# Pair-by-pair loads, earlier product pieces and rest tokens turned together in a fused attention and SwiGLU kernel

## The chip, the cores and the metric

One NeuronCore of a Trainium2 chip runs the whole program. The metric is device time in microseconds (us) from launch to end. TensorE (PE; PEld is its weight load), VectorE (DVE), ScalarE (ACT), GpSimd (POOL) and SyncE (SP) each run their own instructions in order and wait for each other through semaphores. POOL, SP and ACT issue the DMA transfers.

## The reference

Attention over 8 batches of 12 heads, 448 tokens and 64 values per head; then a SwiGLU block over all 3584 tokens:

```python
scores = scale * np.matmul(q, k.transpose(0, 1, 3, 2))
attn = softmax(scores)                      # over the last axis
attn_out = np.matmul(attn, v)               # (8, 12, 448, 64)
x = attn_out.transpose(0, 2, 1, 3).reshape(3584, 768)
g = x @ w_gate                              # (3584, 1536)
out = (g / (1 + exp(-g)) * (x @ w_val)) @ w_out   # (3584, 768), float32
```

## The kernel before

**Tiles.** Two heads make a pair, six pairs a batch, 48 pairs in all (`NHP` = 6, `NPAIR` = 48). The 448 tokens of a head lie as four chunks (`NC`) of 112 partitions (`P`): token 4p + c is row p of chunk c. Queries, keys, values and weights are brought to 16 bits by the load. A *unit* is one chunk of keys of one pair: two score matmuls into a PSUM tile of two banks (`s`) and one exponential of both heads into `E` (`qk`, L213).

**Turning queries and keys.** `prep` (L158) brings a pair's queries and keys into `qkT`, with the 64 values of a head along the partitions. Keys take 448 columns, queries 448 more, and the first 64 query columns are repeated at the end, so that the two heads can read the queries in different rotations (head 0 from column S + D, head 1 from column S). For pair 0 this is done by matmuls against the identity, for pairs 1 to 10 by 16 TensorE transposes and two VectorE copies (L207, L210), from pair 11 on (`NPE`) by DMA transposes on SP from a POOL copy.

**Product with the values.** `pv_chunk` (L229) makes one *piece*: eight matmuls of one chunk of `E` with the values of that chunk, which have a column of ones behind them, so the sums of the softmax come with the product. The product `acc` has seven blocks of 128 rows by 65 columns. In the first six each, 128 tokens of one head; the seventh holds the remaining 64 tokens (the *rest tokens*) of both heads, one head in each half of the partitions. After the fourth piece VectorE takes the reciprocals (L264) and scales into `xt` (L265). For the seventh block, from pair 12 on (`XPE`), two extra VectorE operations (L274) put the halves side by side for the DMA transpose.

**Turning the product.** `turn_x` (L282) turns `xt` into columns of `X`, the input of the FFN (768 rows in six blocks, 896 tokens of two batches). For pairs 0 to 11: three matmuls of 128 columns (L292), two of 64 columns for the rest tokens (L296), and one VectorE copy of 448 columns (L303). For later pairs: two DMA transposes. In `X` the rest tokens of a batch are its first 64 columns.

**FFN.** `ffn1_steps` makes one *visit* per block of 128 hidden columns (12 of them): six matmuls for the gate, a tanh on ScalarE, six matmuls for the value, two VectorE operations (L336, L339). `ffn2_steps` multiplies with `w_out`, ScalarE copies the result to `osb` (L369) and SP writes it out, row piece by row piece (L381), since the order of the tokens in `X` isn't that of the output. In the very last chunk ACT issues the pieces under 64 rows. A block of the FFN is the first 384 columns of an `X` tile, or the other 512.

**PSUM.** `ps_s` has three tiles of two banks, for scores, most gates and the turns of pairs up to 7; `ps_f` has two tiles of one bank, for products, the other turns, the FFN's value side and output, and one gate in visits that have no product. A tile is taken in a ring, so an instruction waits until the tile's user before last is read out.

**Order.** It is written out by hand, each engine keeping the order of the program. The prologue is a loop of 24 units, batch 0's pairs 0 to 5. In it stand the turns of later pairs, loads put into lists by pair (`wq`, issued at the second unit of a pair), value copies (`copy_v`), dummies that keep TensorE at work, pieces from unit 8 on, and `turn_x` of pairs 0 to 3 at the units of `XAT`. Then the loop over `plan` mixes two or three units, products of pairs whose exponentials are made, and FFN visits. The first step makes the last pieces of batch 0 and starts the FFN; the FFN of batch 1's tokens and the rest tokens of batch 0 belong to the second block.

**Loads.** All but the first pair's go through POOL (L127 queries and keys, L134 values, L151 and L153 weights). Each has one of eight semaphores in turn: a load is issued when the load eight earlier has landed. Batch 0's queries and keys are loaded one pair at a time for pairs 1 to 3 and two at a time later, values three pairs at a time:

```python
load_qk16(3, 1)
load_v(0, GP)
load_qk16(4)
load_v(3, GP)
```

Of the kernel before, what the change touches and what calls it, by code (L numbers as in the profile page):

```python
# [23 lines left out]
WIDE = 8  # L24
XPE = 12
NE = 4
NX = 3
NV = 6
VS = 6
EB = 15  # L30


# [1 line left out]
def kernel(  # L34
# [21 lines left out]
    GPB = NHP // GP  # L56
    sm_scale = float(D) ** -0.5
    OH = DM // 2

    tabs = list(get_activation_tables(nc.m.arch).keys())  # L60

# [19 lines left out]
    ps_f = ctx.enter_context(tc.tile_pool(name="ps_f", bufs=2, space=PSUM))  # L81

    Es = [consts.tile([P, NC * EB + 1, D], FP16, name=f"E{i}") for i in range(NE)]
    Xts = [consts.tile([128, 4, 128], FP16, name=f"xt{i}") for i in range(NX)]
    Vts = [consts.tile([P, 2, NC, D + 2], FP16, name=f"vo{i}") for i in range(NV)]
    vraw = consts.tile([P, VS, 2, NC, D], FP16, name="vraw")
    warm = consts.tile([128, 512], FP16, name="warm")
# [51 lines left out]
    def copy_v(pr):  # L139
        nc.vector.tensor_copy(Vts[pr % NV][:, :, :, 0:D], vraw[:, pr % VS])  # L140

# [13 lines left out]
    def prep(pr):  # L155
        rq, rk = raw[pr]
        if pr == 0 or pr >= NPE:
            qk16 = attp.tile([P, 2, NC, 2, D], FP16, tag="qk16", bufs=3)  # L158
            for t, src in enumerate((rq, rk)):
                dst = qk16[:, 1 - t].rearrange("p c h d -> p h c d")  # L160
                if pr == 0:
                    nc.vector.tensor_copy(dst[:, 0], src[:, 0])
                    nc.scalar.activation(dst[:, 1], src[:, 1], AF.Copy)
                else:
                    nc.gpsimd.tensor_copy(dst, src)  # L165
        qkT[pr] = attp.tile([128, 2 * S + D], FP16, tag="qkT", name="qkT", bufs=5)
        if pr >= NPE:
            nc.sync.dma_start_transpose(
                qkT[pr][:, 0 : 2 * S].rearrange("p (c q) -> p c q", q=P),
                qk16[:].rearrange("p t c h d -> p (t c h d)"),  # L170
            )
            nc.sync.dma_start_transpose(
                qkT[pr][:, 2 * S :].rearrange("p (c q) -> p c q", c=1),
                qk16[0:D, 1, 0].rearrange("p h d -> p (h d)"),
            )
            return None

        def turn0():
            for t in range(2):
                tp = ps_s.tile([128, 2, 512], FP32, tag="s", name="tp")  # L180
                for c in range(NC):
                    for hx in range(2):
                        nc.tensor.matmul(
                            tp[ts(hx, 64), c // 2, ds(c % 2 * P, P)],
                            lhsT=qk16[:, 1 - t, c, hx],
                            rhs=ident[0:P, 0:P],
                            start=True,
                            stop=True,
                        )
                dst = qkT[pr][:, ts(1 - t, S)].rearrange("p (a x) -> p a x", a=2)  # L190
                nc.vector.tensor_copy(dst[:, 0], tp[:, 0, 0 : 2 * P])
                nc.scalar.activation(dst[:, 1], tp[:, 1, 0 : 2 * P], AF.Copy)
                if t == 0:
                    tq = tp
            nc.vector.tensor_copy(qkT[pr][:, 2 * S :], tq[:, 0, 0:D])  # L195

        def turn():
            if pr < FIRST + 2:
                tp = ps_s.tile([128, 2 * NC, 256], FP16, tag="s", name="tp")
            else:  # L200
                tp = ps_f.tile([128, 2 * NC, 128], FP16, tag="f", name="tp")
            for t in range(2):
                for c in range(NC):
                    for hx in range(2):
                        src = raw[pr][t][:, hx, c, :]
                        nc.tensor.transpose(tp[ts(hx, 64), (1 - t) * NC + c, 0:P], src, ident[0:P, 0:P])  # L206
            nc.vector.tensor_copy(  # L207
                qkT[pr][:, 0 : 2 * S].rearrange("p (c q) -> p c q", q=P), tp[:, :, 0:P]
            )
            nc.vector.tensor_copy(qkT[pr][:, 2 * S :], tp[:, NC, 0:D])  # L210

        return turn if pr else turn0

# [22 lines left out]
    def pv_chunk(pr, c):  # L236
        if c == 0:
            accs[pr] = ps_f.tile([128, 512], FP32, tag="f", name="acc")
        e = Es[pr % NE]
        vo = Vts[pr % NV]  # L240
        a7 = accs[pr][:, 0 : 7 * (D + 1)].rearrange("p (s d) -> p s d", s=7)
        for j in range(3):
            for hx in range(2):
                nc.tensor.matmul(  # L244
                    a7[:, 2 * j + hx],
                    lhsT=e[:, ds(c * EB + 9 * hx + 2 * j, 2)].rearrange("p b x -> p (b x)"),
                    rhs=vo[:, hx, c, 0 : D + 1],
                    start=c + j + hx == 0,
                    stop=False,
                )  # L250
        for hx in range(2):
            nc.tensor.matmul(  # L252
                a7[:, 6],
                lhsT=e[:, ds(c * EB + 6 + hx, 2)].rearrange("p b x -> p (b x)"),
                rhs=vo[:, hx, c, 0 : D + 1],
                start=False,
                stop=c == NC - 1 and hx == 1,
            )
        if c < NC - 1:
            return  # L260
        r = attp.tile([128, 8], FP32, tag="R", bufs=2, name="R")
        xt = Xts[pr % NX]
        n = 7 if pr < XPE else 6
        nc.vector.reciprocal(r[:, 0:7], a7[:, :, D])  # L264
        nc.vector.tensor_tensor(  # L265
            xt[:].rearrange("p j (h d) -> p (j h) d", h=2)[:, 0:n],
            a7[:, 0:n, 0:D],
            r[:, 0:n].unsqueeze(2).to_broadcast([128, n, D]),
            ALU.mult,
        )  # L270
        if pr < XPE:
            return
        for hx in range(2):
            nc.vector.tensor_scalar(  # L274
                xt[0:D, 3, ts(hx, D)], a7[ts(hx, D), 6, 0:D], r[ts(hx, D), 6:7], None, ALU.mult
            )

    def pv(pr):
# [3 lines left out]
    def turn_x(pr):  # L282
# [6 lines left out]
        if pr < XPE:  # L289
            tp = accs[pr] if pr < FIRST else ps_f.tile([128, 512], FP32, tag="f", name="xtp")  # L290
            for j in range(3):
                nc.tensor.matmul(  # L292
                    tp[:, ds(D + 128 * j, 128)], lhsT=xt[:, j], rhs=ident[:], start=True, stop=True
                )
            for hx in range(2):
                nc.tensor.matmul(  # L296
                    tp[ts(hx, D), 0:D],
                    lhsT=xt[:, 3, 0:D],
                    rhs=ident[:, ts(hx, D)],
                    start=True,  # L300
                    stop=True,
                )
            nc.vector.tensor_copy(dst, tp[:, 0:S])  # L303
            return
        nc.sync.dma_start_transpose(
            dst[:, D:S].rearrange("p (j q) -> p j q", j=3), xt[:, 0:3].rearrange("p j m -> p (j m)")
        )
        nc.sync.dma_start_transpose(dst[:, 0:D].rearrange("p (j q) -> p j q", j=1), xt[0:D, 3])

    gate_small = [False]  # L310

# [32 lines left out]
    def ffn2_steps(kk, c0, n, hts, first, last_block):  # L344
# [6 lines left out]
        for ch, oh in steps:  # L351
# [7 lines left out]
            for m0, w in parts:  # L359
# [15 lines left out]
                l = l0  # L375
                while l < l0 + 128:
                    b, j = divmod(l, S)
                    c, p0 = divmod(j, P)
                    m = min(P - p0, l0 + 128 - l)
                    eng = nc.scalar if last and m < 64 else nc.sync  # L380
                    eng.dma_start(  # L381
                        out[ts(NB * kk + b, S), :].rearrange("(p c) m -> c p m", c=NC)[
# [13 lines left out]
    with tc.manual_schedule():  # L396
# [4 lines left out]
        for vo in Vts:  # L401
            nc.vector.memset(vo[:, :, :, D:], 1.0)
        load_qk16(1, 1)
        make_identity(nc, ident)
        load_qk16(2, 1)
        load_qk16(3, 1)
        load_v(0, GP)
        load_qk16(4)
        load_v(3, GP)
        dummy(7)  # L410
        prep(0)()
# [2 lines left out]

        wq = {
            0: [("qk", 6), ("g", 0), ("v", 0)],
            1: [("qk", 8), ("g", 1), ("v", 1)],
            3: [("qk", 10), ("V", 2), ("g", 2), ("v", 2)],
            4: [("g", 3), ("v", 3), ("qk", 12)],
            6: [("V", 3), ("o", 0)],  # L420
            7: [("o", 1)],
# [30 lines left out]
        def run_o():  # L452
            gen, t = oq.pop(0)
            next(gen)
            return t
# [9 lines left out]
        def share(total, at, n):  # L465
            return (at + 1) * total // n - at * total // n

        XAT = (11, 15, 17, 20)
        pieces = [(p, c) for p in range(FIRST) for c in range(NC)]

        def piece():
# [2 lines left out]
        for u in range(FIRST * NC):  # L474
# [9 lines left out]
                prep(2)()  # L484
            elif u >= 6 and c == 2:
                prep(pr + 2)()
            if u in (5, 6, 7):
                dummy(1)
            if u in (6, 14):
                for p in range(3):  # L490
                    copy_v(u // 8 * 3 + p)
            if c == 1:
                for w in wq.pop(pr, []):
                    emit(w)
            if u in XAT:
                turn_x(XAT.index(u))
            for _ in range(1 if c == 2 or u in XAT else 2):
                if u >= 8 and pieces[0][0] * NC + pieces[0][1] <= u - 3:
                    piece()

        queue = []
# [24 lines left out]
        for x, (chunks, todo) in enumerate(plan):  # L526
# [40 lines left out]
            else:  # L567
# [16 lines left out]
                        run_fv()  # L584
                for _ in range(no):
                    run_o()
            while turns:
                turn_x(turns.pop(0))
        run_budget(1e9)
        oq.extend(ffn2_wait)  # L590
        ffn2_wait.clear()
# [36 lines left out]
```

The softmax here doesn't subtract the row's maximum and nothing guards it: scores larger than these inputs give would overflow.

## Time and profile before

| what | value |
|---|---|
| median of 5 runs (lowest to highest) | 454.06 us (453.71 to 455.16) |
| the profiled execution, its own time | 455.1 us |
| its span, first to last instruction | 453.3 us |
| granted TensorE clock, mean | 0.999 |
| exponentials (L226), 192 | 162.6 us busy |
| FFN gate, value and output matmuls | 124.7, 124.7 and 116.1 us busy |
| products (L244 and L252) | 53.0 and 42.9 us busy |
| scores (L218), 384 matmuls | 50.5 us busy |
| DMA moved | 48.71 MB, mean 107 GB/s |

The share of busy time of an engine is an average over stages that differ: in the first 32 us there is no FFN, in the last 20 no attention. So the timeline is read stage by stage: an engine that is idle shows, in brackets behind its next instruction, for how long and what ended it. The start of a group of equal instructions and the start of the next group give what the first group costs; the printed duration of matmuls includes the way through the array and overlaps with what follows. The landing of a transfer is when its semaphore is raised, counted from the same zero.

The DMA engines are at their rate for the first third of this program (the page's 40 slices are of 11.3 us each):

```profile
DMA  9999999999697839683846737974423102110033
GB/s 131 196 199 201 187 176 160 182 215 133 94 106 105 87 79 159 107 117 82 138 63 120 124 74 119 146 87 78 81 41 78 46 12 80 49 35 1 0 106 104
```

The digits are tenths of the 16 engines' time and the second row is what they moved in each slice.

### The profile page before, as it was taken

Reading aid. Unit: us, or ns where it says so; the run is one execution under the profiler, and the core shown is the slowest. Engines: PE = TensorE matmul, PEld = TensorE weight load, DVE = VectorE, ACT = ScalarE, POOL = GpSimd, SP = SyncE. Lnnn points to the kernel's source line nnn. Section 1 sums busy time; section 2 is a strip of 40 time slices with the busy share of each in tenths; the row PEclk is TensorE's granted clock in tenths of the full one; section 3 lists DMA queues with packets and bytes.
Section 4 is the critical chain, followed back from the end, with each engine's and each line's share of the span. In section 5 each row is a group of like instructions: output and inputs, shape, how many; then the busy total and the mean of one; then the engine's idle time right before and its main releaser. Section 6 shows DMA issues by size and latency. Waiting matters only on the chain.

```text
span 453.3 us, 9845 instructions
## 1 busy us (share of the span) xinstructions
PE 443.9 (98%) x4007; PEld 247.2 (55%) x4007; DVE 200.7 (44%) x456; ACT 239.2 (53%) x350; POOL 138.0 (30%) x222
## 2 busy tenths in 40 slices
PE   8989999999999999999999999999999999999996
PEld 3555655645455656445456665545555656644464
DVE  3655653356563535354443553444354444145400
ACT  6874576766655555645556446644654644222222
POOL 8544715936454325252322504440100000000000
PEclk9999999999999999999999999999999999999999
DMA  9999999999697839683846737974423102110033
GB/s 131 196 199 201 187 176 160 182 215 133 94 106 105 87 79 159 107 117 82 138 63 120 124 74 119 146 87 78 81 41 78 46 12 80 49 35 1 0 106 104
DMA packets 104941, 48.71 MB, mean 107 GB/s; under 512 B 59584, under 2 KB 101440, under 8 KB 104896
## 3 DMA queue, kind: packets, MB, share of 16 engines
q0 software_dynamic: 43296, 23.37, 41.6%
q1 hardware_dynamic: 61504, 24.66, 28.2%
q8 instruction: 31, 0.51, 0.5%
q14 instruction: 14, 0.11, 0.1%
q10 hardware_dynamic: 96, 0.05, 0.0%
HBM read 47.19 MB, written 11.01 MB: 128 GB/s over the span
## 4 chain that ended last, share of the span: by engine, by line
PE 89%; DMA 4%; DVE 2%; ACT 2%; POOL 1%; issue 1%; DVEq 0%; ACTq 0%; POOLq 0%
PE op L362 24%; PE gp L317 23%; PE vp L317 22%; PE acc L244 8%; PE s L218 8%; DMA vraw<-in_v_dram 4%; PE acc L252 2%; ACT E L226 1%; DVE t L336 1%; PE tp L206 1%; POOL k L127 1%; ACT sg L332 1%; DVE qkT L207 0%; POOL q L127 0%; DVE vo L140 0%
## 5 line engine op out<-in xcount | busy, mean ns | idle before, releaser
L226 ACT ACTIVATE E<-s 112x896 f16<-112x896 f32 x192 | 162.6, 918 | 29.9 <-PE s L218 29.2
L317 PE MATMUL vp<-X,wv 128*128 128x384 f16 (+1 forms) x576 | 124.7, 353 | 1.0 <-DVE qkT L210 1.0
L317 PE MATMUL gp<-X,wg 128*128 128x384 f16 (+1 forms) x576 | 124.7, 352 | 0.0
L362 PE MATMUL op<-wo,hts 128*128 128x384 f16 (+1 forms) x684 | 116.1, 323 | 0.0
L336 DVE SCALAR_TENSOR_TENSOR t<-sg,gp 128x384 f32<-128x384 f32 (+1 forms) x96 | 59.6, 621 | 120.5 <-ACT sg L332 120.5
L332 ACT ACTIVATE sg<-gp 128x384 f32<-128x384 f32 (+1 forms) x96 | 52.4, 546 | 85.2 <-PE gp L317 84.0
L362 PEld LDWEIGHTS <-hts 128*128 128x128 f16 x684 | 65.5, 98 | 45.9 <-issue 3.9
L317 PEld LDWEIGHTS <-wv 128*128 128x128 f16 x576 | 56.2, 98 | 53.9 <-DVE qkT L210 1.4
L317 PEld LDWEIGHTS <-wg 128*128 128x128 f16 x576 | 53.0, 97 | 45.7 <-issue 1.1
L369 ACT ACTIVATE osb<-op 128x384 f32<-128x384 f32 (+1 forms) x57 | 27.7, 487 | 92.5 <-PE op L362 88.4
L339 DVE SCALAR_TENSOR_TENSOR hts<-t,vp 128x384 f16<-128x384 f32 (+1 forms) x96 | 59.6, 621 | 11.1 <-PE vp L317 0.8
L165 POOL COPY qk<-q 112x512 f16<-112x512 f16 x37 | 23.0, 621 | 131.1 <-DMA qkT<-qk 129.8
L244 PEld LDWEIGHTS <-E 112*128 112x128 f16 x1152 | 46.3, 97 | 18.5 <-issue 16.6
L244 PE MATMUL acc<-vo,E 112*128 112x65 f16 x1152 | 53.0, 193 | 1.8 <-DVE vo L140 0.7
L218 PE MATMUL s<-qkT 64*128 64x448 f16 x384 | 50.5, 353 | 0.5 <-DVE qkT L195 0.3
L252 PE MATMUL acc<-vo,E 112*128 112x65 f16 x384 | 42.9, 193 | 0.0
L264 DVE RECIPROCAL R<-acc 128x7 f32<-128x7 f32 x48 | 9.8, 205 | 74.2 <-PE acc L252 74.2
L134 POOL DMA_DIRECT2D vraw<-in_v_dram x40 | 26.6, 666 | 29.3 <-DVE vo L140 16.4
L127 POOL DMA_DIRECT2D k<-in_k_dram x42 | 27.8, 661 | 10.8 <-DMA wo<-in_moe_w_out_dram 7.9
L127 POOL DMA_DIRECT2D q<-in_q_dram x42 | 28.0, 666 | 4.5 <-DMA wv<-in_moe_w_val_dram 2.0
L218 PEld LDWEIGHTS <-qkT 64*128 64x128 f16 x384 | 14.7, 94 | 26.4 <-issue 19.6
L265 DVE TENSOR_TENSOR xt<-acc,R 128x384 f16<-128x384 f32 (+1 forms) x48 | 27.6, 574 | 1.7
(42 smaller groups left out, 150.5 us busy)
## 6 DMA issues: line engine op xcount, KB each, us to landing
q<-in_q_dram POOLq DMA_DIRECT2D x37, 112.0 KB, 3.8
k<-in_k_dram POOLq DMA_DIRECT2D x37, 112.0 KB, 4.6
vraw<-in_v_dram POOLq DMA_DIRECT2D x36, 112.0 KB, 4.7
out_dram<-osb SPq DMA_DIRECT2D x7, 336.0 KB, 3.3
wg<-in_moe_w_gate_dram POOLq DMA_DIRECT2D x8, 288.0 KB, 11.3
wv<-in_moe_w_val_dram POOLq DMA_DIRECT2D x8, 288.0 KB, 11.7
wo<-in_moe_w_out_dram POOLq DMA_DIRECT2D x2, 1152.0 KB, 22.4
out_dram<-osb SPq DMA_DIRECT2D x8, 288.0 KB, 3.5
```

The lines of the kernel that those rows point to most:

```text
L127: nc.gpsimd.dma_start(dst[:, ds(h0, 2 * n)], flat.rearrange("h (p c) d -> p h (c d)", c=NC))
L218: nc.tensor.matmul(s[:, hx, 0:S], lhsT=t[ts(hx, 64), c * P : c * P + 128], rhs=t[ts(hx, 64), ds(S + (1 - hx) * D, S)], start=True, stop=True,)
L226: nc.scalar.activation(e[:, :, 0:S], s[0:P, :, 0:S], AF.Exp, scale=sm_scale)
L244: nc.tensor.matmul(a7[:, 2 * j + hx], lhsT=e[:, ds(c * EB + 9 * hx + 2 * j, 2)].rearrange("p b x -> p (b x)"), rhs=vo[:, hx, c, 0 : D + 1] ...
L252: nc.tensor.matmul(a7[:, 6], lhsT=e[:, ds(c * EB + 6 + hx, 2)].rearrange("p b x -> p (b x)"), rhs=vo[:, hx, c, 0 : D + 1], start=False, st ...
L265: nc.vector.tensor_tensor(xt[:].rearrange("p j (h d) -> p (j h) d", h=2)[:, 0:n], a7[:, 0:n, 0:D], r[:, 0:n].unsqueeze(2).to_broadcast([12 ...
L317: nc.tensor.matmul(dst[:, 0:n], lhsT=wslice(kind, fb, cb), rhs=X[kk][:, cb, ds(c0, n)], start=(cb == 0), stop=(cb == NCB - 1),)
L332: nc.scalar.activation(sg[:, 0:n], gp[:, 0:n], AF.Tanh, scale=0.5)
L336: nc.vector.scalar_tensor_tensor(t1[:, 0:n], sg[:, 0:n], 1.0, gp[:, 0:n], ALU.add, ALU.mult)
L339: nc.vector.scalar_tensor_tensor(hts[:, fb, 0:n], t1[:, 0:n], 0.5 * HS, vp[:, 0:n], ALU.mult, ALU.mult)
L362: nc.tensor.matmul(op[:, 0:w], lhsT=hts[:, fb, ts(ch, 128)], rhs=wo[oh][:, fb, ds(m0 - oh * OH, w)], start=(fb == 0), stop=(fb == NFB - 1),)
L369: nc.scalar.activation(osb[:, ds(m0, w)], op[:, 0:w], AF.Copy, scale=1.0 / HS)
```

## The change

Seven things, in the order of the code:

- `turn` makes two more transposes (the first query chunk again) into one contiguous PSUM row of 960 columns, keys ahead of queries, and one VectorE copy takes the place of two.
- `X` has the rest tokens of a batch in its last 64 columns, not its first; the writes of the output follow (`(j + D) % S`, and a cut at `MQ` = 384). A piece of the last chunk that has 64 rows goes through SP.
- `turn_x` of pairs 0 to 11 turns the six blocks of 128 tokens alone. `turn_rests` turns the seventh blocks of a batch's six pairs in twelve matmuls and one VectorE copy: for batch 0 behind the second step of the plan, for batch 1 behind the turn of pair 11.
- `xt` has six buffers of seven blocks, so that the seventh stays; pairs from 12 on have a separate tile `Xrs` for their rest tokens.
- Queries, keys and values of pairs 0 to 5 are loaded in turns of one pair (values of pairs 3 to 5 still together); values of pairs 6 to 8 go ahead of key 8, and pairs 8 and 9 are loaded apart. Nine instead of six places for loaded values, five instead of six for their copies.
- Pieces may start at unit 5; the number per unit changes, the dummies at units 5, 6 and 7 are gone, and the turn of pair 3 is at unit 21.
- Value copies stand one by one, behind the scores of units 4, 7, 11, 14, 17 and 21 (`CAT`), not three at a time at units 6 and 14.

```diff
-NX = 3
-NV = 6
-VS = 6
+NX = 6
+NV = 5
+VS = 9
...
-                tp = ps_s.tile([128, 2 * NC, 256], FP16, tag="s", name="tp")
+                tp = ps_s.tile([128, 2, 1024], FP16, tag="s", name="tp")[:, 0]
             else:
-                tp = ps_f.tile([128, 2 * NC, 128], FP16, tag="f", name="tp")
...
+                tp = ps_f.tile([128, 1024], FP16, tag="f", name="tp")
+            for i in range(2 * NC + 1):
+                t, c = (1 - i // NC, i % NC) if i < 2 * NC else (0, 0)
+                for hx in range(2):
+                    src = raw[pr][t][:, hx, c, :]
+                    nc.tensor.transpose(tp[ts(hx, 64), ts(i, P)], src, ident[0:P, 0:P])
+            nc.vector.tensor_copy(qkT[pr][:], tp[:, 0 : 2 * S + D])
...
-            for hx in range(2):
+            nc.vector.tensor_copy(dst[:, 0:MQ], tp[:, 0:MQ])
+            return
...
+    def turn_rests(b):
+        tp = ps_f.tile([128, NHP, D], FP32, tag="f", name="rtp")
+        for p in range(NHP):
+            for hx in range(2):
                 nc.tensor.matmul(
-                    tp[ts(hx, D), 0:D],
-                    lhsT=xt[:, 3, 0:D],
+                    tp[ts(hx, D), p],
+                    lhsT=Xts[(b * NHP + p) % NX][:, 6],
                     rhs=ident[:, ts(hx, D)],
                     start=True,
                     stop=True,
                 )
-            nc.vector.tensor_copy(dst, tp[:, 0:S])
...
+        nc.vector.tensor_copy(X[0][:, :, b * S + MQ : b * S + S], tp[:])
...
-                    c, p0 = divmod(j, P)
-                    m = min(P - p0, l0 + 128 - l)
+                    c, p0 = divmod((j + D) % S, P)
+                    m = min(P - p0, l0 + 128 - l, (MQ if j < MQ else S) - j)
...
+        load_v(0)
         load_qk16(3, 1)
-        load_v(0, GP)
-        load_qk16(4)
+        load_v(1)
+        load_qk16(4, 1)
+        load_v(2)
+        load_qk16(5, 1)
         load_v(3, GP)
...
-            1: [("qk", 8), ("g", 1), ("v", 1)],
-            3: [("qk", 10), ("V", 2), ("g", 2), ("v", 2)],
+            1: [("V", 2), ("qk", 8, 1), ("g", 1), ("v", 1)],
+            3: [("qk", 9, 1), ("qk", 10), ("g", 2), ("v", 2)],
...
-        XAT = (11, 15, 17, 20)
+        XAT = (11, 15, 17, 21)
+        CAT = (4, 7, 11, 14, 17, 21)
...
-            if u in (5, 6, 7):
-                dummy(1)
-            if u in (6, 14):
-                for p in range(3):
-                    copy_v(u // 8 * 3 + p)
...
+            if u in CAT:
+                copy_v(CAT.index(u))
             if u in XAT:
                 turn_x(XAT.index(u))
-            for _ in range(1 if c == 2 or u in XAT else 2):
-                if u >= 8 and pieces[0][0] * NC + pieces[0][1] <= u - 3:
+            for _ in range(2 if c == 3 else int(c != 2 or u > 12)):
+                if u >= 5 and pieces[0][0] * NC + pieces[0][1] <= u - 3:
                     piece()
...
+            if x == 1:
+                turn_rests(0)
             while turns:
                 turn_x(turns.pop(0))
+            if XPE - 1 in [p0 for _, p0 in todo]:
+                turn_rests(1)
```

More of the change, by code (lines that the diff above doesn't have):

```diff
@@ L58 @@
     OH = DM // 2
+    MQ = S - D
     tabs = list(get_activation_tables(nc.m.arch).keys())
@@ L83 @@
     Es = [consts.tile([P, NC * EB + 1, D], FP16, name=f"E{i}") for i in range(NE)]
-    Xts = [consts.tile([128, 4, 128], FP16, name=f"xt{i}") for i in range(NX)]
+    Xts = [consts.tile([128, 7, D], FP16, name=f"xt{i}") for i in range(NX)]
+    Xrs = [consts.tile([D, 128], FP16, name=f"xr{i}") for i in range(3)]
     Vts = [consts.tile([P, 2, NC, D + 2], FP16, name=f"vo{i}") for i in range(NV)]
@@ L198, in turn @@
             if pr < FIRST + 2:
-                tp = ps_s.tile([128, 2 * NC, 256], FP16, tag="s", name="tp")
+                tp = ps_s.tile([128, 2, 1024], FP16, tag="s", name="tp")[:, 0]
             else:
-                tp = ps_f.tile([128, 2 * NC, 128], FP16, tag="f", name="tp")
-            for t in range(2):
-                for c in range(NC):
-                    for hx in range(2):
[L205 to L210, printed above, removed]
+                tp = ps_f.tile([128, 1024], FP16, tag="f", name="tp")
[5 more added lines that the diff above has]
+            nc.vector.tensor_copy(qkT[pr][:], tp[:, 0 : 2 * S + D])
         return turn if pr else turn0
@@ L262, in pv_chunk @@
         xt = Xts[pr % NX]
+        nc.vector.reciprocal(r[:, 0:7], a7[:, :, D])
         n = 7 if pr < XPE else 6
-        nc.vector.reciprocal(r[:, 0:7], a7[:, :, D])
         nc.vector.tensor_tensor(
-            xt[:].rearrange("p j (h d) -> p (j h) d", h=2)[:, 0:n],
+            xt[:, 0:n],
             a7[:, 0:n, 0:D],
@@ L274, in pv_chunk @@
             nc.vector.tensor_scalar(
-                xt[0:D, 3, ts(hx, D)], a7[ts(hx, D), 6, 0:D], r[ts(hx, D), 6:7], None, ALU.mult
+                Xrs[pr % 3][:, ts(hx, D)], a7[ts(hx, D), 6, 0:D], r[ts(hx, D), 6:7], None, ALU.mult
             )
@@ L292, in turn_x @@
                 nc.tensor.matmul(
-                    tp[:, ds(D + 128 * j, 128)], lhsT=xt[:, j], rhs=ident[:], start=True, stop=True
-                )
+                    tp[:, ts(j, 128)],
+                    lhsT=xt[:, 2 * j : 2 * j + 2].rearrange("p h d -> p (h d)"),
+                    rhs=ident[:],
+                    start=True,
+                    stop=True,
+                )
+            nc.vector.tensor_copy(dst[:, 0:MQ], tp[:, 0:MQ])
+            return
+        nc.sync.dma_start_transpose(
+            dst[:, 0:MQ].rearrange("p (j q) -> p j q", j=3),
+            xt[:, 0:6].rearrange("p j d -> p (j d)"),
+        )
+        nc.sync.dma_start_transpose(dst[:, MQ:S].rearrange("p (j q) -> p j q", j=1), Xrs[pr % 3][:])
+    def turn_rests(b):
+        tp = ps_f.tile([128, NHP, D], FP32, tag="f", name="rtp")
+        for p in range(NHP):
             for hx in range(2):
                 nc.tensor.matmul(
-                    tp[ts(hx, D), 0:D],
-                    lhsT=xt[:, 3, 0:D],
+                    tp[ts(hx, D), p],
+                    lhsT=Xts[(b * NHP + p) % NX][:, 6],
                     rhs=ident[:, ts(hx, D)],
@@ L302, in turn_x @@
                 )
-            nc.vector.tensor_copy(dst, tp[:, 0:S])
[L304 to L308, printed above, removed]
+        nc.vector.tensor_copy(X[0][:, :, b * S + MQ : b * S + S], tp[:])
     gate_small = [False]
```

## The prediction

> **What bounds the kernel now.** I read the page first (shares, chain), then TensorE's waits, then the timeline of the first 45 us and of the last 5.
>
> ```profile
> PE 443.9 (98%) x4007; PEld 247.2 (55%) x4007; DVE 200.7 (44%) x456; ACT 239.2 (53%) x350; POOL 138.0 (30%) x222
> ...
> PEclk9999999999999999999999999999999999999999
> ...
> PE 89%; DMA 4%; DVE 2%; ACT 2%; POOL 1%; issue 1%; DVEq 0%; ACTq 0%; POOLq 0%
> ```
>
> TensorE sets the end; the 4% of DMA in the chain is all `vraw`, the load of the values. TensorE's waits of the first 100 us are all it has:
>
> ```profile
> PE acc L292 <- DVE xt L265: 1.3, 2, 1.0
> ...
> PE vp L317 <- DVE qkT L210: 1.0, 1, 1.0
> PE acc L244 <- DVE vo L140: 0.7, 1, 0.7
> PE acc L244 <- DVE t L336: 0.5, 1, 0.5
> ```
>
> The timeline shows where they lie (start, duration, engine, operation, idle time before it and what ended it):
>
> ```profile
> 13.21 0.70 DVE L140 COPY vo<-vraw 112x512 f16<-112x512 f16 x3 [0.84 <-DMA vraw<-in_v_dram]
> ...
> 13.56 0.35 PE L244 MATMUL acc<-vo,E 112*128 112x65 f16 x6 [0.72 <-DVE vo L140]
> ...
> 14.56 1.80 ACT L226 ACTIVATE E<-s 112x896 f16<-112x896 f32 x2 [0.57 <-PE s L218]
> ...
> 32.29 0.34 PE L292 MATMUL acc<-ident,xt 128*128 128x128 f16 x3 [0.96 <-DVE xt L265]
> ...
> 32.72 1.15 PE L317 MATMUL gp<-X,wg 128*128 128x384 f16 x6
> ...
> 38.89 0.29 DVE L140 COPY vo<-vraw 112x512 f16<-112x512 f16 x1 [1.30 <-DMA vraw<-in_v_dram]
> ...
> 39.87 1.15 PE L317 MATMUL vp<-X,wv 128*128 128x384 f16 x6 [1.00 <-DVE qkT L210]
> ```
>
> Up to 13.5 us the exponentials go back to back (0.81 us apart) and TensorE fills its spare time with dummies; pieces cannot start, since the values of pairs 0 to 2 come in one load that lands at 13.19. From 14 us on TensorE is late and ScalarE idles. The FFN starts at 32.72; at 38.87 it stops for 1.00 us behind a value copy whose load was issued at 28.33 and landed at 38.87.
>
> **Prologue, worked through by TensorE's order.** Start-to-start costs of a unit, from before's rows: scores and one piece 0.64 (24.82 to 25.46), and two pieces 0.885 (14.15 to 15.03); scores, turn of 16, one piece 1.16 (27.54 to 28.70); a turn of X with its rest pair, scores and a piece 1.07 (16.28 to 17.35), of which the rest pair is 0.15 (16.85 to 17.00). As a check, these and the 0.66 us of waits give 15.04 for before's units 9 to 23; the trace has 15.20. In the changed kernel a turn has 18 transposes, 0.03 each: +0.06 (so 0.87 without a piece, 1.22 with one); the turn of X loses the rest pair (0.91, or 1.15 with two pieces).
>
> Unit 5 starts at 9.92 as before (two early turns could add 0.1). Its piece waits for the first value copy: VectorE's copy of `qkT` starts at 9.96, takes 0.66 (0.62 scaled from 896 columns), the value copy 0.29, so TensorE is free at 11.0, if the load has landed by 10.65. It is now fifth on POOL's queue, and the fifth load of before landed at 9.62. Unit 6 starts at 11.36 (before 10.72, with dummies). Then by the order of the changed program: units 6 to 10 cost 0.87, 0.885, 0.64, 0.64, 0.87; 11 to 15: 1.15, 0.64, 0.64, 1.22, 1.15; 16 to 20: 0.64, 0.91 and 0.2 of waiting for `xt` of pair 2, 1.22, 0.885, 0.64; 21 to 23: 0.91, 1.22, 0.64. Sum 15.97, so unit 24 is at 27.33, not 29.35. ScalarE keeps up: an exponential starts 0.40 after its scores and 0.81 after the one before, and only units 11 and 14 come within 0.1 of its limit. Two scores 0.58, `xt` of pair 4 late by 0.13, its turn 0.27, then as before 1.85 from the first of the last three pieces to the last turn (30.44 to 32.29; reciprocal and scale stand there in both), 0.27: FFN at 30.43. With 0.1 for the early turns: **-2.2 us**. VectorE takes 2.3 us per pair of 3.7, so it hides its copies; the one copy instead of two (0.80 to 0.66) matters only ahead of unit 5's piece.
>
> **Loads.** POOL gets six more transfers (0.66 us of issue each) but waits for landings from 11.8 us on, so these lie in its idle time. The next keys (third pair, before 10.18) fall into the place where the first third of the values was: 10.18 plus a third of 3.0 makes 11.2, needed at 11.65. Later loads end at the same bytes. The values of pairs 6 to 8 go ahead of keys 8 and weights 1 and should land near 28, needed at 35: the stall at 38.87 goes, **-1.0**; what is late next there, the copy of `qkT`, ends 0.1 before TensorE wants it. Weights 1 land 0.6 later (35.4, needed at 39.6). Here a rule of the Trainium skill speaks against the change: "DMA: Bandwidth & Descriptors", section "Bandwidth", wants large transfers, as each pays some 2 us of fixed cost ("Anatomy of one DMA"). Six more would be 12 us if they stood in line. The rows say otherwise: two-head loads in flight land 0.56 to 0.65 us apart (8.97, 9.62, 10.18), four-head loads 1.17 to 1.21. The fixed cost lies under the others; I take 0.
>
> **Rest tokens.** Batch 0's twelve small matmuls move behind the second FFN visit. No row has twelve in line: two take 0.15 (0.075 each) with the change of form; alternating transposes take 0.03 each. Ends 0.4 and 0.9; I take 0.45, the nearer row being the alternating one. Their PSUM slot is the gate's, freed by VectorE's L336, 0.3 after TensorE gets there: **+0.75** (0.4 to 1.4), with scores and pair 6's product queued behind. Pairs 6 to 11 lose their rest pair: 6 x 0.15 = **-0.9**. Batch 1's twelve cost 0.45, and wait for the copy of the FFN's output to free the slot (ScalarE 0.49, of which 0.27 under the turn of X): 0.45; **+0.9** (0.4 to 1.4). Turns of pairs 8 to 10: **+0.18**. The new VectorE copies (384 columns, some 0.55) end before the next user of their slot.
>
> **The dummies** at units 5 to 7 go (0.21 each on TensorE, in time it had free). The skill ("TensorE: Matmul & The Clock Gate", Part 1) has the clock fall to half after an idle window of about 3.4 us. The row: granted clock 1.00 in 0 to 10 and 10 to 20, across a pause of 0.73. By the rule's worst case a half-rate window would add up to 3.4; the longest new pause is 0.8, so I take 0.
>
> **Tail.** The last rows were written by two queues at once (SP and ACT, 450.16 and 450.17, landed 451.88 and 452.04); now SP issues both halves, 0.38 apart: **+0.3** (0 to 0.6). The other stages keep their instructions; in them TensorE had no wait to lose. More and differently cut output writes on SP (0.42 each) lie beside its idle time.
>
> Sum: -2.2 - 1.0 + 0.75 - 0.9 + 0.9 + 0.18 + 0.3 = **-2.0**. The profiled execution took 455.1 (span 453.3 and 1.8 around it), so its like would be 453.1; the median shown, 454.06, lies 1.0 below it: **452.1**.
>
> **Rivals.**
> (a) The gain is half lost (-0.9 to +0.9, near 453.6): keys of pair 3 or values 1 late by 0.5 to 1 each, or the two rest groups at their upper ends (+1.1 over my sum). For it: 6.5 to 8 us moved only 27 to 45 KB per 0.5 us where 80 to 95 is usual, so landings there are uneven. Against: most have 0.5 us and more to spare.
> (b) Slower: the value load of pair 0 comes late. Its piece now stands ahead of unit 6's scores in TensorE's order, so ScalarE dries up too; before, it stood behind unit 8's. Every microsecond past 10.65 costs one. Landing at 12.65 eats the gain, and from 13.6 on the kernel is slower by over 0.2%; at 14, 455.4 to 455.5. For it: the load that it replaces (three pairs) landed at 13.19. Against: it is a third of that and two places earlier.
> (c) The clock falls for one window: +3.4 - 2.0, near 455.5.
> (d) The order is better than I reckon: no stall at the rest groups and the wait of 0.49 at 59.85 gone: -3.2, 450.9.
>
> **How the numbers follow.** Forecast 0.61 (451.2 to 453.1), (a) 0.20, (b) 0.09, (c) 0.03, (d) 0.07. Two runs of this kernel tell 0.2% (0.9 us) from nothing, so faster means under 453.15. Faster: 0.59 of the forecast, 0.07 of (d) and little of (a): 0.67; same: most of (a), 0.18; slower: (b), (c) and the rest of (a), 0.15. The range goes from 450.9 to 454.3, into (a) but not to (b).
>
> **What would show it.** First piece near 11.0 and FFN start near 30.4; no wait for values at the third visit; a gap of about 0.3 ahead of each rest group; the end 0.3 later after the last copy; clock 1.00. Wrong if the first piece waits for its load past 11.5, if scores start over 0.9 us apart while ScalarE idles between units 6 and 13, or if FFN stages after 100 us show new waits.

## The result, and the profile after

| | before | after |
|---|---|---|
| median of all timed runs (lowest to highest) | 454.44 us (453.27 to 459.27, 79 runs) | 453.29 us (452.97 to 453.87, 44 runs) |
| ratio, 95% interval | | 0.9973 (0.9966 to 0.9980) |
| profiled execution, its own time | 455.1 us | 453.24 us |
| its span | 453.3 us | 451.4 us |
| granted TensorE clock, mean | 0.999 | 0.997 |

The kernel is faster by 0.27%, some 1.2 us from median to median; the forecast was 2.0. The page of after, by the rows that were shown of before (busy time, share of the span and number of instructions; the clock in 40 slices; the chain by engine):

```profile
PE 441.6 (98%) x4024; PEld 247.0 (55%) x4024; DVE 203.2 (45%) x447; ACT 238.8 (53%) x350; POOL 141.6 (31%) x228
...
PEclk9999999999999999999999999999999999999998
...
PE 94%; ACT 2%; DVE 2%; issue 0%; DVEq 0%; ACTq 0%
```

The loads have left the chain (DMA had 4% of it), and TensorE is busy for 2.3 us less. What it still waits for in the first 100 us (us in total, times, longest):

```profile
PE acc L291 <- DVE xt L264: 1.0, 1, 1.0
PE acc L243 <- DVE vo L142: 0.6, 1, 0.6
PE acc L243 <- DVE t L345: 0.4, 1, 0.4
PE rtp L310 <- ACT osb L378: 0.4, 1, 0.4
...
PE tp L208 <- DVE hts L348: 0.2, 1, 0.2
PE rtp L310 <- DVE t L345: 0.2, 1, 0.2
```

The wait of `vp` for `qkT` is gone; two waits ahead of the rest groups (`rtp`) are new, and a third of 0.2 us ahead of the turn of pair 9 (`tp` for `hts`). The timeline, with the same columns as before:

```profile
10.91 0.34 PE L243 MATMUL acc<-vo,E 112*128 112x65 f16 x6 [0.58 <-DVE vo L142]
...
29.34 0.34 PE L291 MATMUL acc<-ident,xt 128*128 128x128 f16 x3 [0.96 <-DVE xt L264]
29.52 1.14 PE L326 MATMUL gp<-X,wg 128*128 128x384 f16 x6
...
35.55 1.14 PE L326 MATMUL vp<-X,wv 128*128 128x384 f16 x6
36.88 0.38 PE L310 MATMUL rtp<-ident,xt 128*64 128x64 f16 x12 [0.19 <-DVE t L345]
37.19 0.55 PE L217 MATMUL s<-qkT 64*128 64x448 f16 x4
```

The first piece starts at 10.91 instead of 13.56. The FFN starts at 29.52 instead of 32.72: 3.2 us gained. At the scores that follow the third visit (37.19, before 40.95) the gain is 3.76, though the first rest group lies within it. Behind the second rest group it is 3.50, and it stays at that until the copy of the last output, which ends at 446.66 instead of 450.14. These rows, first of before for the scores, then of before and after for the last copy, show both:

```profile
40.95 0.55 PE L218 MATMUL s<-qkT 64*128 64x448 f16 x4
...
449.81 0.33 ACT L369 ACTIVATE osb<-op 128x192 f32<-128x192 f32 x1 [0.56 <-PE op L362]
...
446.33 0.33 ACT L378 ACTIVATE osb<-op 128x192 f32<-128x192 f32 x1 [0.61 <-PE op L371]
```

The span is shorter by 1.9 only. So 1.6 us were lost behind the last copy. The queue of SP there in after: the line's duration of one issue (lowest, median, highest, in ns), first and last start, number; then issue to landing:

```profile
L390 SPq DMA_DIRECT2D out_dram<-osb x6: 472/571/598, 444.9 to 448.0; - x6
...
DMA to landing us min/median/max: 1.9/2.0/2.2
```

In before, the last six:

```profile
L381 SPq DMA_DIRECT2D out_dram<-osb x3: 316/316/317, 448.4 to 450.2; - x3
L381 ACTq DMA_DIRECT2D out_dram<-osb x3: 375/377/392, 448.4 to 450.2; - x3
```

In before the last two issues start 0.02 and 0.03 us behind the last copy, and the span ends 3.2 us behind that copy. In after SP issues six writes of 64 rows, one behind the other, 0.5 to 0.7 apart. The last starts at 448.00, 1.3 us behind the copy, and the span ends 4.8 behind it.

### The profile page after: what moved, and what is told of

Same layout as the page of the kernel before. It is cut to its first block, busy times and chain, and to the rows that moved or that the text cites. A ratio compares the mean times of both kernels' runs of the same rounds, so it can differ in the third digit from the quotient of the medians.

```text
span 451.4 us, 9871 instructions
## 1 busy us (share of the span) xinstructions
PE 441.6 (98%) x4024; PEld 247.0 (55%) x4024; DVE 203.2 (45%) x447; ACT 238.8 (53%) x350; POOL 141.6 (31%) x228
## 4 chain that ended last, share of the span: by engine, by line
PE 94%; ACT 2%; DVE 2%; issue 0%; DVEq 0%; ACTq 0%
PE op L371 24%; PE gp L326 23%; PE vp L326 23%; PE acc L243 9%; PE s L217 9%; PE acc L251 3%; ACT E L225 2%; PE tp L208 1%; PE wp L109 1%; DVE t L345 1%; ACT sg L341 1%; PE acc L291 0%; DVE qkT L209 0%; DVE xt L264 0%; DVE hts L348 0%
## 5 line engine op out<-in xcount | busy, mean ns | idle before, releaser
L129 POOL DMA_DIRECT2D k<-in_k_dram x44 | 28.9, 658 | 9.3 <-DMA wo<-in_moe_w_out_dram 8.1
L129 POOL DMA_DIRECT2D q<-in_q_dram x44 | 29.2, 664 | 4.9 <-PE s L217 2.5
L136 POOL DMA_DIRECT2D vraw<-in_v_dram x42 | 28.0, 666 | 7.9 <-DVE vo L142 6.9
```

Of the source, the lines that this page charges most:

```text
L129: nc.gpsimd.dma_start(dst[:, ds(h0, 2 * n)], flat.rearrange("h (p c) d -> p h (c d)", c=NC))
L136: nc.gpsimd.dma_start(vraw[:, ds(pr % VS, n)].rearrange("p r h c d -> p (r h) (c d)"), v[b, h : h + 2 * n].rearrange("h (p c) d -> p h (c ...
```

## Experiments

Each kernel was timed in alternation with the kernel before on one chip. There were four groups of runs on four chips, with before's median at 454.45, 454.51, 454.30 and 454.16, so ratios are compared, not microseconds. After's own ratio is 0.9973.

Where two profiles are compared, one thing must come off first: executions differ already at the first units, where the programs are still the same, by up to 2 us (the last section shows why). So a difference is counted from the point where the programs part.

**The tail: two queues.** After, with the second half of each of the last pieces on ACT:

```diff
-eng = nc.scalar if last and m < 64 else nc.sync
+eng = nc.scalar if last and j >= MQ else nc.sync
```

> The changed kernel, with the rest half (64 rows) of the very last chunk's writes issued by ACT instead of SP. Theory (SP's six writes of 64 rows in a row, 0.47 to 0.60 each, end 1.3 us behind the last copy): both last writes are issued at once, so the end comes 1.3 us earlier after the last copy, near 452.0 where the changed kernel has 453.3. Rival (the landing of small writes sets the end, whoever issues them): less than 0.4 earlier.

Measured: 452.85 (452.36 to 454.47, 12 runs), 0.9973 (0.9961 to 0.9985); no gain in the median. The trace does show one. ACT in after, then in this kernel:

```profile
444.40 0.49 ACT L378 ACTIVATE osb<-op 128x384 f32<-128x384 f32 x1 [1.51 <-PE op L371]
445.39 0.33 ACT L378 ACTIVATE osb<-op 128x192 f32<-128x192 f32 x1 [0.50 <-PE op L371]
...
444.77 0.49 ACT L378 ACTIVATE osb<-op 128x384 f32<-128x384 f32 x1 [1.51 <-PE op L371]
445.29 0.55 ACTq L390 DMA_DIRECT2D out_dram<-osb  x1
445.96 0.33 ACT L378 ACTIVATE osb<-op 128x192 f32<-128x192 f32 x1 [0.71 <-PE op L371]
```

This execution is 0.37 late ahead of the tail (444.77 for 444.40), and has been since unit 18 of the prologue. ACT's issue stands between its own copies, but delays the next one by only 0.20 more (445.96 for 445.39). The last two issues start 0.02 and 0.03 behind the last copy, the last landing follows it by 2.2 us (after: 3.3), and the span ends 3.7 behind it instead of 4.8. So the line of issues was the cause: a second queue takes 1.1 of the 1.6 away, 0.9 when the delay of the copies is taken off. The median hides it, since the runs fall into two groups: seven at 452.36 to 452.95, with the profiled one, and five at 453.87 to 454.47.

**The tail: other row counts.** All on SP, the last block's chunks in another order, so that the last pieces have 96 and 32 rows:

```diff
-chunks = range(n // 128)
+chunks = (0, 3, 2, 1) if last_block else range(n // 128)
...
-eng = nc.scalar if last and m < 64 else nc.sync
+eng = nc.sync
```

> The changed kernel, with the chunks of the last FFN block in the order 0, 3, 2, 1, so that the very last chunk is written in pieces of 96 and 32 rows, all by SP. Theory (SP's writes of 64 rows take 0.47 to 0.60 and queue up; pieces of other sizes take 0.31 to 0.43 and are issued before the next copy ends): the last write is issued 0.4 after the last copy instead of 1.3, so 0.9 to 1.0 earlier, 452.3, with the narrow spread of the changed kernel. Rival (landing sets it): 453.3.

Measured: 452.17 (451.77 to 453.93, 7 runs), 0.9954 (0.9937 to 0.9970). The same six issues:

```profile
L390 SPq DMA_DIRECT2D out_dram<-osb x6: 317/396/442, 446.4 to 448.7; - x6
```

From the last copy to the end of the span it takes 3.5 us instead of 4.8. So one queue is enough when its issues are shorter: what cost the 1.3 us was six issues of 64 rows in one line, and either way out, a second queue or other row counts, removes most of it. Before's trace held the row for it: two 64-row writes at 438.6 and 439.2.

```profile
L381 SPq DMA_DIRECT2D out_dram<-osb x2: 497/535/573, 438.6 to 439.2; - x2
```

**The tail of before on one queue.** Meant to see whether ACT's writes at the end make the runs of before scatter.

```diff
-eng = nc.scalar if last and m < 64 else nc.sync
+eng = nc.sync
```

> The kernel before, with the small pieces of the very last chunk issued by SP instead of ACT. Its runs lie 2.2 us apart (453.75 to 456.01 in the last job), those of the changed kernel 0.9; the changed kernel with ACT's writes lay 2.1 apart, in two groups. Theory (writes by ACT at the end land late in some executions): the runs come within 1 us of each other, the median at 454.2 to 454.6 (0.4 of a second issue against the lost outliers). Rival (the spread comes from the loads of the prologue): the spread stays at 2 us.

Measured: 455.01 (453.61 to 458.10, 12 runs), 1.0018 (0.9999 to 1.0036). The scatter stays; that theory falls. But the kernel tests the tail too: its last six issues stand in one line on SP with 16 and 112 rows, 0.31 to 0.41 each. The last starts 0.48 behind the last copy, and the span ends 3.5 behind it, where before has 3.2. That is the 0.3 that the prediction gave to a single queue.

**Value loads of the prologue together.** Values of pairs 0 to 2 in one load behind keys 3, pieces still from unit 5:

```diff
-load_v(0)
 load_qk16(3, 1)
-load_v(1)
+load_v(0, GP)
 load_qk16(4, 1)
-load_v(2)
```

> The changed kernel, with the values of pairs 0 to 2 in one load behind the keys of pair 3, as before; pieces still from unit 5. Theory (the first piece stands ahead of unit 6's scores in TensorE's order and waits for the landing at 13.2): first piece at 13.5 instead of 10.9 and the whole 2.6 us kept to the end, near 455.9, slower than before. Rival (the prologue has room to catch up): up to 1.0 over the changed kernel, 454.3.

Measured: 458.69 (455.74 to 459.44, 6 runs), 1.0075 (1.0051 to 1.0098). Timeline:

```profile
13.62 0.29 DVE L142 COPY vo<-vraw 112x512 f16<-112x512 f16 x1 [2.77 <-DMA vraw<-in_v_dram]
13.96 0.34 PE L243 MATMUL acc<-vo,E 112*128 112x65 f16 x6 [3.45 <-DVE vo L142]
14.70 1.82 ACT L225 ACTIVATE E<-s 112x896 f16<-112x896 f32 x2 [2.99 <-PE s L217]
```

The load landed at 13.6, the piece waited 3.45 us with the scores of unit 6 queued behind it, and ScalarE dried up for 2.99. That is +3.05 at the first piece, near what rival (b) gives (13.6 less 10.65 is 2.95). Then the clock fell (a stretch, its length, busy time of PE, PEld, DVE, ACT and POOL, granted clock, DMA):

```profile
15.00:20.00 5.00, 5.00 (x68) 3.14 (x62) 1.80 (x4) 4.18 (x5) 4.01 (x6) 0.53 1.38 199
```

By unit 13 it had cost another 2.7 us; the span is longer by 5.4. The one timed run with the clock at 1.000 took 455.74, 0.2 under the expectation, which reckoned with no fall of the clock; those at 0.988 to 0.991 took 458.5 to 459.4. The split of the loads carries the change; without it the earlier pieces make the kernel slower.

**Pieces from unit 8 again,** with the dummies at 5 to 7 and before's count per unit:

```diff
+if u in (5, 6, 7):
+    dummy(1)
...
-    if u >= 5 and pieces[0][0] * NC + pieces[0][1] <= u - 3:
+    if u >= 8 and pieces[0][0] * NC + pieces[0][1] <= u - 3:
```

> The changed kernel, with pieces from unit 8 on, the old number of pieces per unit, and the dummies at units 5 to 7. Theory (TensorE's own work sets the prologue from unit 8 on, and each piece made earlier in dummy time is won): the FFN starts some 1.2 us later, 454.5. Rival (ScalarE's exponentials set it): within 0.3 of the changed kernel.

Measured: 453.71 (453.40 to 454.46, 11 runs), 0.9980 (0.9971 to 0.9990): +0.3 us in the ratio, which the intervals do not part from after. The profile is 0.8 longer, all of it in the prologue. But 0.36 of that stands at unit 4, where the programs are the same (after, then this kernel):

```profile
9.03 0.36 PE L217 MATMUL s<-qkT 64*128 64x448 f16 x2
...
9.39 0.36 PE L217 MATMUL s<-qkT 64*128 64x448 f16 x2
```

That leaves 0.44. The direction is the theory's; the size is about a third of its 1.2, nearer to the rival's 0.3.

**Values of pairs 6 to 8 late again,** in after:

```diff
-1: [("V", 2), ("qk", 8, 1), ("g", 1), ("v", 1)],
-3: [("qk", 9, 1), ("qk", 10), ("g", 2), ("v", 2)],
+1: [("qk", 8, 1), ("g", 1), ("v", 1)],
+3: [("qk", 9, 1), ("qk", 10), ("V", 2), ("g", 2), ("v", 2)],
```

> The changed kernel, with the load of the values of pairs 6 to 8 put back to its old place behind the keys of pairs 10 and 11. Theory (the prologue's gain and this load are not a sum: the load lands near 38.9 whatever TensorE does, and the third FFN visit now stands at 34.6, so nearly all that the prologue won is waited away there): a stall of 4.0 to 4.4 us, near 457.5. Rival (the terms add up, as the prediction added them): the stall of 1.0 comes back, 454.3.

Measured: 459.18 (456.97 to 459.93, 6 runs), 1.0093 (1.0075 to 1.0112).

```profile
39.02 2.08 PE L326 MATMUL vp<-X,wv 128*128 128x384 f16 x6 [3.06 <-DVE qkT L209]
```

```profile
38.00:45.00 7.00, 5.98 (x57) 3.40 (x57) 2.98 (x7) 1.72 (x2) 2.99 (x4) 0.52 1.32 202
45.00:50.00 5.00, 4.80 (x47) 2.92 (x45) 2.99 (x7) 1.85 (x4) 3.92 (x6) 1.00 1.36 199
```

TensorE stands for 3.06 us at the place where before stood for 1.00, since the prologue ends 3 us earlier and the load lands only 0.8 earlier (38.08 for 38.87). The six matmuls then take 2.08 instead of 1.15: half rate, until 45. The prologue's gain and the earlier values are not two gains that add: without the second, the first is lost to the wait and to the clock, which cost 2.4 us more behind the wait.

**Values of pairs 6 to 8 early, in before:**

```diff
-VS = 6
+VS = 9
...
-1: [("qk", 8), ("g", 1), ("v", 1)],
-3: [("qk", 10), ("V", 2), ("g", 2), ("v", 2)],
+1: [("V", 2), ("qk", 8), ("g", 1), ("v", 1)],
+3: [("qk", 10), ("g", 2), ("v", 2)],
```

> The kernel before, with one part of the change alone: the values of pairs 6 to 8 loaded ahead of the keys of pair 8 (and nine places for loaded values). Theory (the stall of 1.00 at 38.87 is this load and nothing is right behind it): 1.0 faster than before, 453.4. Rival (another wait takes its place, such as the copy of the keys behind it): under 0.3.

Measured: 454.15 (453.63 to 457.38, 12 runs), 0.9997 (0.9982 to 1.0011). The stall is gone from its profile, but the median moved by 0.1 to 0.4 and not by 1.0. The one-queue tail of before, whose prologue is before's, shows a reason; its stall was half as long:

```profile
39.39 1.15 PE L317 MATMUL vp<-X,wv 128*128 128x384 f16 x6 [0.48 <-DVE qkT L210]
```

The same load, 10.5 us under way in both, was there 0.5 earlier. So the stall of 1.00 was that of one execution. The profiled run of this kernel (454.90) does not settle it, for it had a late start: it is 0.74 behind before when the FFN starts and 0.42 ahead behind the third visit, 1.2 won at the very place. How long the stall is on average stays open: two profiles, and a scatter of the runs as large as the effect.

**Rest tokens turned pair by pair,** as before:

```diff
-nc.vector.tensor_copy(dst[:, 0:MQ], tp[:, 0:MQ])
+for hx in range(2):
+    nc.tensor.matmul(tp[ts(hx, D), MQ:S], lhsT=xt[:, 6], rhs=ident[:, ts(hx, D)], start=True, stop=True)
+nc.vector.tensor_copy(dst, tp[:, 0:S])
...
-turn_rests(0)
...
-turn_rests(1)
```

> The changed kernel, with each pair's rest tokens turned in that pair's own turn of X again (two small matmuls per pair, copy of 448 columns) and no group of twelve. In the changed kernel's trace the two groups cost 0.31 each and wait 0.19 and 0.41 (1.22 in all). Theory (twelve pairs of small matmuls at 0.15 each stand on TensorE, of which the six in the prologue count too, as TensorE sets it): 1.8 - 1.2 = 0.6 later, 453.9. Rival (ScalarE hides those of the prologue): 0.9 - 1.2, so 0.3 earlier, 453.0.

Measured: 454.62 (453.79 to 455.92, 12 runs), 1.0001 (0.9990 to 1.0013), slower than after by the intervals. The runs fall into three groups: 453.79 to 454.12, 454.62 to 454.80 and 455.57 to 455.92. The profiled one is the highest and had the late start that is told of at the end. Its trace gives the size all the same: it is 1.92 behind after at unit 11, ahead of the first turn of X; 3.45 when the FFN starts, so that the prologue's six rest pairs cost 0.25 each; and 2.71 from the place of the second rest group to the last copy. The pairs one by one cost 0.8 more than the groups, where the theory had 0.6.

**The turn of queries and keys with 16 transposes and two copies,** as before:

```diff
-for i in range(2 * NC + 1):
+for t in range(2):
+    for c in range(NC):
...
+nc.vector.tensor_copy(qkT[pr][:, 2 * S :], tp[:, NC, 0:D])
```

> The changed kernel, with the old turn of queries and keys: 16 transposes into a padded PSUM tile and two VectorE copies (896 and 64 columns). Theory (TensorE sets the time, and a pair of transposes costs 0.05 to 0.06, ten times): 0.3 to 0.6 earlier, 452.7 to 453.0. Rival (the second copy of 0.18 delays the first piece and the values behind it): 0.2 later, 453.5.

Measured: 452.77 (452.47 to 454.39, 12 runs), 0.9968 (0.9955 to 0.9982). The interval does not part it from after. In the trace it is 0.17 ahead of after at unit 0, where the programs are the same, and 0.45 from the last turn on. The ten turns so account for 0.28: 0.05 at a turn where they show, near the 0.06 reckoned, and nothing at the others. No gain from the single copy is seen.

**Two further versions.** Both stand on the kernel with 96 and 32 rows at the end. One puts a dummy between the halves of pair 0's turn, the other moves `turn_rests` behind the scores of the next step:

```diff
+                    dummy(1)
```

```diff
+            if rests:
+                turn_rests(rests.pop())
...
-                turn_rests(0)
+                rests.append(0)
...
-                turn_rests(1)
+                rests.append(1)
```

> As e8, with one more dummy matmul between the two halves of pair 0's turn. In the profiles with a late start (E8's among them) TensorE pauses 0.32 to 0.36 there, the matmuls run at half rate to 9.4 to 10.2 us and everything from unit 2 on is 1.5 us late; in the others there is no such pause and full rate comes at 4.1 to 6.1. Theory (the pause keeps the clock's window from counting as busy): no run in the later group, all within 1.0 us, median 452.2 to 452.5 (the dummy costs up to 0.3 where there was no pause). Rival (the group is drawn otherwise, by where the window falls): again two groups 1.5 apart.

> As e8, with both groups of rest tokens moved from the end of a step behind the scores of the next one, ahead of its product. Theory (their waits of 0.19 and 0.41 are for a PSUM tile that is read out while the scores run): 0.5 to 0.6 less than e8, 451.6 in the early group. Rival (the tile is then missed by the product or the gate behind it): as e8, 452.2.

The dummy: 452.63 (452.01 to 452.89, 6 runs), 0.9961 (0.9948 to 0.9975), no better than without it. All runs lie within 0.9 us, as the theory has it, but after's 44 runs do so without a dummy, so six more runs show little. The profile, with the full rate at 6.70 us, is 0.96 behind after from unit 6 on; the theory allowed the dummy 0.3.

The rests behind the scores: 451.36 (451.25 to 451.79, 5 runs), 0.9939 (0.9926 to 0.9953), the lowest median of all, though its interval still overlaps that of the 96 and 32 rows alone. In the trace it gains 0.64 on after between unit 6 and the last copy, and both `rtp` waits (0.19 and 0.41) are gone:

```profile
36.69 0.55 PE L217 MATMUL s<-qkT 64*128 64x448 f16 x4
37.17 0.38 PE L310 MATMUL rtp<-ident,xt 128*64 128x64 f16 x12
```

The twelve matmuls follow the scores with no wait: the PSUM slot has come free while these ran. With the turn of 16 added:

> E11 with the old turn of 16 transposes of E7. Theory (both act on TensorE's own work and waits, in different places, so they add up): 0.5 under E11, 450.9 in the early group. Rival (the second copy on VectorE now stands in front of the rest group's copy and its slot): as E11, 451.4.

Measured: 451.94 (450.87 to 452.71, 6 runs), 0.9951 (0.9935 to 0.9966), in two groups near 451.2 and 452.6. It has the lowest single time of all, but its median shows no gain over the version without it. The trace does: from unit 6 to the last copy it gains 0.94 on after, where the rests alone gain 0.64 and the turn of 16 alone 0.30, so that the two add up.

## Why the prediction held, and where its sum was off

The time (453.29) lies in the range and on the side forecast, but past the forecast's own 451.2 to 453.1, near rival (a)'s 453.6, and not for (a)'s reasons: no load was late, and the rest groups cost less than reckoned. That the profiled executions lie 1.9 apart, next to the 2.0, is luck: up to the last copy the sum was -2.3 and the trace gave -3.5; behind it +0.3 and +1.6. Two terms were mis-sized, with opposite signs.

- **Prologue: -2.2, measured -3.2.** The first piece came at 10.91 (forecast 11.0), its load landed at 9.10 against 10.65 needed, so rival (b) had 1.5 us to spare. Units without a turn of X came out within 0.03 of their forecast costs. Too dear by 0.1 each were the six turns of X (1.05 instead of 1.15 with two pieces), since a rest pair costs 0.25 there, not 0.15; the waits for `xt`, 0.20 and 0.13 in the sum, came to 0.1 together; 0.1 more was the first piece. Together 0.9; the rest is the 0.1 set aside for the early turns. By the runs, 1.5 of the 3.2 are the six rest pairs and 0.4 the earlier pieces. No run takes the remaining 1.2 or so apart: the value copies one by one and the turn at unit 21 were never tested alone.
- **Values of pairs 6 to 8: -1.0.** The load landed at 27.79 (forecast 28) and the wait went, as said. The size was one execution's: 0.48 in another. The sum started from a profiled execution 1.0 above the median shown, kept that distance, and took off its whole stall of 1.0. This is one part of why the profiles differ by 1.9 and the medians by 1.2; before's profile lies 0.7 above the median of its 79 runs.
- **Small loads at no cost.** The first values landed at 9.10, 11.11 and 12.99, between keys 0.5 to 0.9 apart. The rule weighed against the rows, that each transfer pays its own fixed cost, would have spoken for one load; that version lost 5 us. (Rival (a)'s uneven stretch from 6.5 to 8 us holds; the trace has 25 to 52 KB per 0.5 us there, and 68 to 86 around it.)
- **Rest tokens of batch 0: +0.75, measured +0.5** (0.19 of waiting and 0.31 for twelve; they stand behind the third visit, not the second). **Batch 1: +0.9, measured +0.72** (0.41 and 0.31). Twelve such matmuls cost what alternating transposes cost, 0.026 each.
- **Rest pairs of pairs 6 to 11: -0.9, measured some -0.6.** One did cost 0.15 (56.23 to 56.38 in before), but the new wait of 0.20 ahead of the turn of pair 9 takes part of it back. The gain went from 3.76 to 3.50 there, with 0.72 and 0.15 lost to the second rest group and the turns of 18.
- **Turns of 18: +0.18, measured 0.15**, 0.05 each. The kernel would be better without them.
- **Dummies: 0.** Right in result. The reason was half empty: "granted clock 1.00 in 0 to 10" says nothing of the first microseconds (see the end). What held was that no pause passed 0.96. The worst case was too small in duration: after pauses of 3.06 and 3.45 us half rate lasted 6.8 us, not 3.4; in time lost it was 2.4 and 2.7, under the 3.4 taken.
- **Tail: +0.3, measured +1.6. This is the step that failed.** It took the spacing of other SP issues (0.38) for one pair. One queue with 16 and 112 rows does cost 0.3, as the tail of before on one queue shows. But the rows in the last chunk are 64 and 64, whose issues take 0.47 to 0.60, and there are six in a row. Both could be read from before: two 64-row writes of 0.50 and 0.57, and three copies in the last 3 us, each with two writes behind it.

## What to carry to other kernels

When a stage starts earlier, look at which transfer it then meets first: splitting and reordering the loads were worth more than the moved work, for without one of them the kernel took 4.6 or 5.4 us more (by the ratios) than with both. Price an issue on a queue by a row with the same number of rows, and count how many stand in line behind the last producer. A wait seen in one execution is worth its mean over executions, not its length in that profile; and a small group that waits for a buffer belongs behind the next work that needs none. Line two profiles up at a place ahead of the first difference between the programs before reading a difference of less than 2 us from them.

## What the runs showed of the hardware

**Issue time by rows.** Behind 425 us, in the fourteen traces together, the 64 writes of 64 rows on SP took 0.47 to 0.60 us to issue. Those of 16, 32, 48, 80, 96 and 112 rows took 0.31 to 0.45, but for eleven of 48 rows at 0.57. Why 64 rows are dearer is open.

**The clock stays at half for 6.8 us.** In the two runs with pauses of 3.06 and 3.45 us the clock records show half rate for 6.8 us. In the first it fell at 38.22, 2.3 us into the pause; in the second at 15.34, 1.4 us after work had begun again. The Trainium skill ("TensorE: Matmul & The Clock Gate", Part 1) gives about 3.4 us as the window in which idling closes the gate, and at least one busy window of the same length to open it; here a pause under 3.4 closed it, and it took twice that to open.

**The clock at the start differs between executions.** The view of windows gives a clock of 1.00 from the first microsecond, but the first clock record comes only when the full rate is granted. That was at 4.67 us in after and 5.15 in before, and by 6.8 in eleven of the fourteen profiles; in the other three it was at 9.35, 10.19 and 10.22. Until then matmuls run at half rate: in after, dummies start 0.43 apart before 4.67, and 0.23 apart at 8.49. In the kernel with 96 and 32 rows (9.35):

```profile
4.39 0.70 PE L185 MATMUL tp<-ident,qk 112*64 112x112 f16 x8
5.41 0.58 PE L185 MATMUL tp<-ident,qk 112*64 112x112 f16 x8 [0.32 <-DVE qk L164]
...
6.61 0.93 PE L217 MATMUL s<-qkT 64*128 64x448 f16 x4
```

and in after:

```profile
4.29 1.11 PE L185 MATMUL tp<-ident,qk 112*64 112x112 f16 x16
...
6.02 0.62 PE L217 MATMUL s<-qkT 64*128 64x448 f16 x4 [0.29 <-DVE qkT L197]
```

Four scores take 0.93 instead of 0.62, and at unit 6 the three late profiles are 1.5 to 1.9 us behind after or before. What decides is open. In two of the three TensorE paused for 0.32 and 0.36 between the halves of pair 0's turn, but in the third (values of pairs 6 to 8 early, in before) it did not pause there at all, so the pause alone, which the expectation of the dummy run took for common to all three, isn't the cause. All three come from one group of runs, on one chip, whose fourth profile had the full rate at 4.21; the chip as a cause was not tested. In the three the first queries landed at 3.98 to 4.02 us, in the other eleven at 3.22 to 3.93, which is a lead and no more.

This start would explain the groups of runs in several kernels, 1 to 1.5 us apart; that rests on these profiles, as timed runs have no trace. It leaves one thing unexplained: none of after's 44 runs lies in an upper group, though kernels with the same beginning have such runs.
